# Turning Q and K of the first two batches with full 128x128 transposes, in runs of four rows

## The chip, the cores and the metric

The kernel runs on one core of a Trainium2 chip. The metric is device time in microseconds (us) of one execution, as a median over several executions. TensorE is PE in the profile (PEld is its weight load), VectorE is DVE, ScalarE is ACT, GpSimd is POOL, and SyncE is SP; on this kernel nearly every transfer is issued from SP.

## The reference, cut to what matters

Eight batches of eight heads, 576 positions and 64 values per head go through attention with a window of 32 positions on either side, and the result through a layer that squares a ReLU.

```
scores = (q @ k.T) / sqrt(64)                    # q, k, v: (8, 8, 576, 64), f32
scores = where(abs(i - j) <= 32, scores, -1e9)
attn   = softmax(scores)
x      = (attn @ v), heads side by side          # (4608, 512)
h      = x @ w_in                                # (512, 2048)
out    = (s * relu(h)**2 + b) @ w_out            # (2048, 512) -> (4608, 512), f32
```

## The kernel before, in words

All matrix work is in bf16. Heads go in four pairs: a pair has its two heads' 64 values on partitions 0 to 63 and 64 to 127. Positions go in nine tiles of 64 queries or keys, and two tiles make a unit (five units per batch, the last with one tile). The window of 32 makes each key tile meet 128 query positions.

**The plan.** No engine's order is written out by hand. `add` (line 88) records tasks with an engine, a cost, what they read and write, and a key (a due time); `plan` (line 119) then simulates the engines with those costs and fixes, for each engine, one order; `emit` (line 227) gives each engine its instructions in that order, with the semaphore waits that the data needs. Each engine then works strictly down its list. The costs in the code are the planner's; they are no measurements. A changed cost, key or dependency in one place can therefore move instructions on every engine, far away too.

**Q and K of batches 0 and 1.** `load_pair` (617) loads one pair of Q or of K: each partition takes nine consecutive rows of one head, 2304 bytes in a run, into a staging buffer STG (eight of them in a ring, which the weights use too). `turn_pair` (626) casts it to bf16 (ACT, DVE or POOL; lines 630 and 631), turns it on PE by 18 transposes of 64x64 (637, nine for each half of the partitions) into one of the two halves of the accumulator W, and copies it to QT (ACT, 643) or KT (DVE, 644), which puts the rows back in order. The same two halves of W take the outputs of the first layer.

**Scores of batches 0 and 1.** `pair_scores` (851) computes the scores of a pair, 16 products for tiles 0 to 7; tile 8 goes to the accumulator AVN in batch 0 and through `qk_part` (725) in batch 1. In batch 0 the accumulator is first filled with the mask by a product (860, 866); in batch 1 the mask is multiplied in afterwards (897). `first_exp` (890) takes the exponential. `av_part` (767) multiplies by V (785), `finish` (799) divides by the row sums (807, 809), turns the result by four 128x128 transposes (816) and copies it into XT (824).

**V of batch 0** comes in runs of four rows (586), is cast (590) and put into place by products (605); its last 64 rows come apart (570, 64 partitions with eight runs of 256 bytes).

**The two layers.** `s1` (1011) is the first layer for one block of tokens (96, 128, 128, 160, 256, 256, then 512) and a group of features: products with w_in into a half of W (1022), ReLU on ACT (1029), square on DVE (1031). The order of the first four blocks is the list FIRST. `early` (1063) is the second layer of those four blocks (1071, 64 products), and also holds the column sums of w_out (1080, 1084, 1087, 1089), which need all of w_out. `s2` (1035) is the second layer of the later blocks (1040). The weights come in 16 loads of 512 KB (542); POOL casts them (545). POOL also makes the masks for the later batches (474, 479, 509, 512), which wait for the last product with V of batch 0.

**What is done when.** Head (to about 26 us): loads, batch 0's attention. Then the first layer of the first four blocks, while POOL casts weights. From 41 us: the column sums, the second layer of the first blocks, and batch 1's attention among it, since its turns have the due time of batch 1's tokens (972 to 981). From 65 us: the two layers back to back, with the later batches' attention among them; those are turned by DMA transposes (683).

Of the kernel before, what the change touches and what calls it, by code (L numbers as in the profile page):

```python
# [11 lines left out]
S = 576  # L12
D = 64
H = 8
# [14 lines left out]
ORDER0 = (("r", 0), ("r", 1), ("w", 0), ("v", NUNIT - 1), ("w", 1), ("w", 2), ("w", 3))  # L29
ROWE = ("pool", "dve")  # L30
WINE = ("pool", "pool", "pool", "pool")
FIRST = ((0, 0), (1, 0), (2, 0), (0, 1), (1, 1), (2, 1), (3, 0), (3, 1), (0, 2), (1, 2), (2, 2), (3, 2), (0, 3), (1, 3), (2, 3), (3, 3))
WOUTE = (("pool", "pool"),) * 4
ORDER1 = (("w", 0), ("w", 1), ("w", 2), ("w", 3), ("p", 0), ("p", 1), ("p", 2), ("p", 3),
          ("v", 0), ("v", 1), ("v", 2), ("v", 3), ("v", 4))
SWITCH = 215.0
XTS = 4000.0
ROWS = 9
# [8 lines left out]
BANK1 = ("W", "SC", "SC", "AVN", "AVN")  # L47
# [271 lines left out]
def bass_sliding_window_symmetric__then__act_starrelu_kernel(  # L319
# [23 lines left out]
    with ExitStack() as es:  # L343
# [257 lines left out]
        def place_v():  # L601

            grid = PICK.rearrange("p a r -> p (a r)")
            where = [(W, "W", 0), (W, "W", 1), (SC, "SC", 0), (SC, "SC", 1)]
# [12 lines left out]
        def load_pair(b, name, pr, load_key):  # L617

            si = take("stg", NSTG)
            land["pair", b, name, pr] = si  # L620
            add("sp", lambda e: e.dma_start(
                STG[si][:, 0:576],
                src_of[name][b, 2 * pr:2 * pr + 2, :, :].rearrange("h (p i) d -> (h p) (i d)", i=ROWS)),
                600.0, writes=[("STG", si)], key=load_key, dma=("l", 8, 113.0 if b == 0 else 93.0))

        def turn_pair(b, name, pr, key, banks, eng, slack):

            slot, si, ni = b % 2, land["pair", b, name, pr], take("nat", NNAT)
            nat = NAT[ni][:, 0:576]
            add(eng, (lambda e: e.copy(nat, STG[si][:, 0:576])) if eng == "act" else  # L630
                (lambda e: e.tensor_copy(nat, STG[si][:, 0:576])),
                {"act": 670.0, "dve": 420.0, "pool": 700.0}[eng], reads=[("STG", si)], writes=[("NAT", ni)],
                key=key, slack=slack)
            res, tile = banks[take("bank", len(banks))]
            view = tile.bitcast(BF16)[:, 0:S].rearrange("p (i s) -> p i s", i=ROWS)
            order = view.rearrange("p i s -> p s i")
            add("pe", [lambda e, i=i, p0=p0: e.transpose(  # L637
                view[p0:p0 + 64, i, :], nat[p0:p0 + 64, i * 64:i * 64 + 64], IDENT[p0:p0 + 64, p0:p0 + 64])
                for i in range(ROWS) for p0 in (0, 64)], 400.0, reads=[("NAT", ni), "IDENT"], writes=[res], key=key)
            land["turn", b, name, pr] = g.tasks[-1]  # L640
            flat = QT[slot][:, pr, WIN:WIN + S] if name == "q" else KT[slot][:, pr, :]
            dst = flat.rearrange("p (s i) -> p s i", i=ROWS)
            add(*(("act", lambda e: e.copy(dst, order), 190 + 0.833 * S) if name == "q" and (b, pr) not in TURN_DVE else
                  ("dve", lambda e: e.tensor_copy(dst, order), 60 + 1.04 * S)), reads=[res],  # L644
                writes=[({"q": "QT", "k": "KT"}[name], slot, x, pr) for x in range(NTILE)], key=key)
# [117 lines left out]
        def av_banks(b, u):  # L763
            name = ("O", "AVN", "SC", "O", "AVN")[u] if b == 0 else BANK1[u] if b == 1 else "AVN"
            return {"SC": SC, "O": O, "AVN": AVN, "W": W}[name], [(name, 0), (name, 1)]

        def av_part(b, u):
# [8 lines left out]
            def put(h, x, g):  # L776
# [7 lines left out]
                buf, c = (ex if j // 2 == u else px), 64 * (i - j)  # L784
# [8 lines left out]
            near = {pi} if not tiles(b, u) else {ei, pi} if u > 0 else {ei}  # L793
            reads = [("E", x, hp, pr) for x in near for hp in (0, 1) for pr in range(NPAIR)]
# [56 lines left out]
        def pair_scores(b, pr):  # L851
# [3 lines left out]
            whole = range(NTILE - NTILE % 2)  # L855
            tail = [NTILE - 1] if b == 0 and NTILE % 2 else []
            if b == 0:
                wide = NEG.rearrange("p (one c) -> p one c", one=1)
                four = wide.to_broadcast((128, 4, 128))
                add("pe", [lambda e, hp=hp: e.matmul(bank[:, hp, :].rearrange("p (a c) -> p a c", a=4), lhsT=IDENT[:, :],  # L860
                                                     rhs=four, start=True, stop=True, skip_group_check=True)
                           for hp in (0, 1)], 440, reads=[("NEG", 0), ("NEG", 64), "IDENT"], writes=[(name, 0), (name, 1)], key=-80.0 + pr,
                    waits=[land["turn", 0, "k", pr - 1]] if pr else [])
                if pr == 0:
                    half = wide[0:64].to_broadcast((64, 4, 128))
                    add("pe", [lambda e, hp=hp: e.matmul(
                        AVN[0:64, hp, :].rearrange("p (a c) -> p a c", a=4), lhsT=IDENT[0:64, 0:64],
                        rhs=half, start=True, stop=True, skip_group_check=True) for hp in (0, 1)],
                        440, reads=[("NEG", 0), ("NEG", 64), "IDENT"], writes=[("AVN", 0), ("AVN", 1)], key=-79.5)
            fns = [lambda e, j=j, hp=hp: e.matmul(  # L870
                bank[64 * (j % 2):64 * (j % 2) + 64, hp, 64 * (j - j % 2):64 * (j - j % 2) + 128] if j in whole else
# [57 lines left out]
        def attention():  # L929
# [16 lines left out]
            for name, t in ORDER0:  # L946
# [3 lines left out]
                elif name == "r":  # L950
                    load_rows(t, nxt())
                else:
                    w("in", t)
# [416 lines left out]
```

## Time and profile before

| | |
|---|---|
| median of 3 runs | 318.66 us (318.14 to 320.07) |
| the profiled execution's own time | 317.79 us |
| its span, first to last instruction | 316.0 us |
| PE busy | 304.2 us (96%) |
| DVE, ACT, POOL busy | 192.6, 141.9, 89.4 us |
| PE idle, 0 to 30 us | 6.8 us |
| PE idle, 120 to 200 us | 0.0 us |
| mean granted PE clock | 0.984; 0.50 from 16.5 to 26 us |
| DMA, 16 to 37 us | 365 to 400 GB/s |

The profile is of one execution. Its page gives busy time, the span in 40 slices, the chain of work that ended last, and the costliest groups of instructions; the trace behind it answers for any stretch. Two cautions on reading it: PE's instructions are pipelined and their ends are modelled, so one matmul's duration (a 128x128 transpose is shown with 219 ns) is longer than what it adds to a row of its kind; the chain shows the latter. And a wait for several semaphores is put down to the one that came last.

### The profile page before, as it was taken

The numbers are of one execution on the slowest core, as the hardware profiler recorded it, in microseconds if no ns is written. First come the engines' busy times: TensorE is split into PE (matmuls) and PEld (weight loads), VectorE is DVE, ScalarE is ACT, GpSimd is POOL, SyncE is SP. The second block draws the span as 40 slices with busy tenths as digits, with TensorE's granted clock in tenths as the row PEclk, the third lists the DMA queues.
The fourth block names the chain that finished last, engine by engine and source line by source line (L and its number), as shares of the span: only waits on it lengthen the run. The fifth ranks groups of instructions, "written<-read, shape, count | busy, mean of one in ns | idle before, by whom it ended". The sixth has DMA issues, their size and how long they took to land.

```text
span 316.0 us, 8489 instructions
## 1 busy us (share of the span) xinstructions
PE 304.2 (96%) x3618; PEld 163.7 (52%) x3618; DVE 192.6 (61%) x383; ACT 141.9 (45%) x221; POOL 89.4 (28%) x108
## 2 busy tenths in 40 slices
PE   8669999989999999999999999999999999999996
PEld 3349875466764454554444444444444444444444
DVE  4455676488894885788479477786445543333312
ACT  3645435355744674764166354444444333333300
POOL 3377965427135135233312501260000000000000
PEclk9958999999999999999999999999999999999999
DMA  7999998997997998899999799974221110000122
GB/s 258 343 373 387 353 233 260 153 193 238 251 182 176 294 183 171 281 193 144 255 253 167 159 250 281 170 161 122 65 64 51 52 46 35 33 35 33 36 92 79
DMA packets 95881, 56.13 MB, mean 178 GB/s; under 512 B 69920, under 2 KB 85024, under 8 KB 95840
## 3 DMA queue, kind: packets, MB, share of 16 engines
q1 hardware_dynamic: 95840, 55.56, 74.0%
q8 instruction: 29, 0.48, 0.7%
q14 instruction: 12, 0.10, 0.1%
HBM read 36.70 MB, written 9.44 MB: 146 GB/s over the span
## 4 chain that ended last, share of the span: by engine, by line
PE 90%; POOL 5%; issue 2%; DVE 1%; ACT 0%; POOLq 0%
PE w L1022 37%; PE o L1040 35%; PE avn L785 4%; POOL wout L545 3%; PE sc L727 2%; PE w L637 2%; PE avn L1071 2%; PE o L1071 2%; PE avn L816 1%; PE sc L785 1%; POOL win L545 1%; PE o L785 1%; PE sc L870 1%; PE sc L860 0%; DVE kt L644 0%
## 5 line engine op out<-in xcount | busy, mean ns | idle before, releaser
L1022 PE MATMUL w<-xt,win 128*128 128x512 bf16 (+4 forms) x832 | 144.6, 316 | 0.0
L1029 ACT ACTIVATE r<-w 128x512 bf16<-128x512 f32 (+2 forms) x148 | 86.6, 586 | 105.4 <-PE w L1022 87.2
L1040 PE MATMUL o<-wout,gt 128*128 128x512 bf16 (+1 forms) x528 | 126.5, 373 | 0.0
L1031 DVE TENSOR_TENSOR gt<-r 128x512 bf16<-128x512 bf16 (+2 forms) x148 | 77.5, 527 | 77.2 <-ACT r L1029 76.7
L1022 PEld LDWEIGHTS w<-xt,win 128*128 128x128 bf16 x832 | 69.8, 99 | 53.0 <-issue 0.6
L1040 PEld LDWEIGHTS o<-wout,gt 128*128 128x128 bf16 x528 | 50.7, 98 | 55.0
L693 POOL COPY kt<-ktr 128x512 bf16<-128x512 bf16 (+1 forms) x30 | 32.2, 1074 | 38.0 <-DMA ktr<-nat 36.6
L676 POOL CAST nat<-stg 128x1024 bf16<-128x1024 f32 (+1 forms) x21 | 23.5, 1118 | 61.5 <-DMA stg<-in_q_dram 36.3
L755 ACT ACTIVATE ex<-sc 128x1024 bf16<-128x1024 f32 (+1 forms) x29 | 29.7, 1023 | 23.9 <-PE avn L785 21.9
L1056 DVE SCALAR_TENSOR_TENSOR outs<-o,sb,cvec 128x512 f32<-128x512 f32 (+1 forms) x35 | 25.4, 729 | 14.0 <-PE o L1040 13.9
L759 DVE TENSOR_TENSOR ex<-ex,mask 128x1024 bf16<-128x1024 bf16 (+1 forms) x29 | 22.2, 767 | 1.6 <-ACT ex L755 0.5
L809 DVE TENSOR_TENSOR xn<-avn,rec 128x512 bf16<-128x512 f32 (+1 forms) x32 | 22.1, 690 | 1.0
L785 PE MATMUL avn<-vb,ex 64*64 64x65 bf16 x976 | 21.0, 200 | 0.4
L785 PEld LDWEIGHTS avn<-vb,ex 64*64 64x64 bf16 x976 | 13.7, 109 | 13.5 <-issue 8.2
L676 DVE CAST nat<-stg 128x1024 bf16<-128x1024 f32 (+1 forms) x15 | 13.0, 866 | 0.6 <-DMA stg<-in_k_dram 0.6
L727 PE MATMUL sc<-qt,kt 64*64 64x128 bf16 x440 | 11.7, 216 | 0.0
L579 DVE CAST vb<-vst 128x512 bf16<-128x512 f32 (+1 forms) x28 | 11.5, 416 | 0.0
L824 ACT COPY xt<-avn 128x512 bf16<-128x512 bf16 (+2 forms) x15 | 7.7, 521 | 7.3 <-PE avn L816 7.3
L807 DVE RECIPROCAL rec<-avn 128x8 f32<-128x8 f32 (+1 forms) x32 | 6.4, 201 | 6.2 <-PE avn L785 6.2
L1071 PE MATMUL o<-wout,gt 128*128 128x512 bf16 x32 | 9.1, 380 | 0.0
L545 POOL CAST wout<-stg 128x1024 bf16<-128x1024 f32 x8 | 8.8, 1101 | 0.5
L1071 PE MATMUL avn<-wout,gt 128*128 128x512 bf16 x32 | 8.9, 381 | 0.0
(100 smaller groups left out, 144.1 us busy)
## 6 DMA issues: line engine op xcount, KB each, us to landing
out_dram<-outs SPq DMA_DIRECT2D x35, 256.0 KB, 2.6
vst<-in_v_dram SPq DMA_DIRECT2D x28, 256.0 KB, 5.3
stg<-in_q_dram SPq DMA_DIRECT2D x6, 1024.0 KB, 6.0
stg<-in_k_dram SPq DMA_DIRECT2D x6, 1024.0 KB, 10.7
stg<-in_moe_w_in_dram SPq DMA_DIRECT2D x8, 512.0 KB, 10.8
stg<-in_moe_w_out_dram SPq DMA_DIRECT2D x8, 512.0 KB, 9.7
stg<-in_q_dram SPq DMA_DIRECT2D x8, 288.0 KB, 4.5
stg<-in_k_dram SPq DMA_DIRECT2D x8, 288.0 KB, 4.1
```

The lines of the kernel that those rows point to most:

```text
L676: add(eng, lambda e, x=x: e.tensor_copy(nat[0:top, 1024 * x:1024 * x + 1024].rearrange("p (i h d) -> p h i d", h=H, i=2), stg[0:top, :].re ...
L693: add("pool", lambda e, c=c, w=w: e.tensor_copy(KT[slot][:, :, c:c + w].rearrange("p a (s i) -> p a s i", i=4), KTR[slot][:, :, :, c // 4: ...
L755: add("act", lambda e, dst=flat_dst, src=flat_src: e.activation(dst, src, AF.Exp, bias=0.0, scale=0.125), 190 + 0.833 * 512 * len(hs), rea ...
L759: add("dve", lambda e, flat=flat, mask=mask: e.tensor_tensor(flat, flat, mask, ALU.mult), 130 + 0.53 * 512 * len(hs), reads=[("E", ei, hp, ...
L785: return [lambda e: e.matmul(av[64 * x:64 * x + 64, h, 0:D + 1], lhsT=buf[64 * g:64 * g + 64, h % 2, h // 2, c:c + 64], rhs=VB[64 * g:64 * ...
L809: add("dve", lambda e: e.tensor_tensor(XN[xi][0:p1, :].rearrange("p (a c) -> p a c", a=H), av[0:p1, :, 0:D], REC[ri][0:p1, :].rearrange("p ...
L1022: add("pe", [lambda e, g=g, kc=kc: e.matmul(wt[:, g, :], lhsT=WIN_BF[:, kc, (f0 + g) * 128:(f0 + g + 1) * 128], rhs=XT[:, kc, t0 % XR:t0 % ...
L1029: add("act", lambda e: e.activation(rt, wt, AF.Relu, bias=0.0, scale=1.0), 190 + 0.833 * ng * nt, reads=[("W", wb)], writes=[("R1", rb)], ...
L1031: add("dve", lambda e: e.tensor_tensor(GT[gs][:, f0:f0 + ng, g0:g0 + nt], rt, rt, ALU.mult), 130 + 0.53 * ng * nt, reads=[("R1", rb)], wri ...
L1040: add("pe", [lambda e, fc=fc: e.matmul(O[:, ob, 0:cn], lhsT=GT[gs][:, fc, g0:g0 + 128], rhs=WOUT_BF[:, fc, c0:c0 + cn], start=(fc == 0), s ...
L1056: add("dve", lambda e: e.scalar_tensor_tensor(OUTS[us][:, 0:cn], bank, SB128[:, 0:1], CVEC[:, c0:c0 + cn], ALU.mult, ALU.add), 200 + 1.07 ...
L1071: add("pe", [lambda e, fc=fc, bank=bank, gs=gs, g0=g0: e.matmul(bank, lhsT=GT[gs][:, fc, g0:g0 + 128], rhs=WOUT_BF[:, fc, :], start=(fc == ...
```

## The change

Each partition now takes four consecutive rows of both heads of a pair, so that positions 0 to 511 of a pair load as 128 partitions with two runs of 1024 bytes. The cast swaps the order to row, head, value, so that one full 128x128 transpose turns one row of every run for both heads: four transposes a tensor and pair instead of 18. Positions 512 to 575 of all heads come apart (`load_rest`): Q's 64 rows on partitions 0 to 63 and K's on 64 to 127, in eight runs of 256 bytes each, into the free half of a staging buffer (that of K, pair 3 in batch 0; that of Q, pair 0 in batch 1). Their two loads wait for that buffer's own load. POOL casts them, `turn_rest` turns them by four transposes into W, and two copies (both on ACT in batch 0, both on DVE in batch 1) bring them to QT and KT.

The scores of a pair are now tiles 0 to 6 only (14 products). Tiles 7 and 8 of all pairs are computed together by `last_scores` (16 products and one exponential of 128x1024 a batch), in AVN for batch 0 and in both halves of W for batch 1, and `av_part` takes both tiles from there. Some accumulators of the units change places.

Batch 1 is no longer taken up after the first layer of the first four blocks, but in four steps among its last passes (TURN in FIRST), with the due time -17.5; the column sums are recorded ahead of FIRST.

```
-ORDER0 = (("r", 0), ("r", 1), ("w", 0), ("v", NUNIT - 1), ("w", 1), ("w", 2), ("w", 3))
+ORDER0 = (("r", 0), ("r", 1), ("e", 0), ("w", 0), ("v", NUNIT - 1), ("w", 1), ("w", 2), ("w", 3))
-FIRST = (..., (3, 2), (0, 3), (1, 3), (2, 3), (3, 3))
+TURNKEY = -17.5
+TURN = (None, 0)
+FIRST = (..., (3, 2), TURN, (0, 3), TURN, (1, 3), TURN, (2, 3), TURN, (3, 3))
+TAIL = ("act", "dve")
+HOST = (("k", 3), ("q", 0))
+REST = ("pool", "pool")
-          ("v", 0), ("v", 1), ("v", 2), ("v", 3), ("v", 4))
+          ("v", 0), ("v", 1), ("e", 0), ("v", 2), ("v", 3), ("v", 4))
-ROWS = 9
+ROWS = 4
+BODY = 128 * ROWS
-BANK1 = ("W", "SC", "SC", "AVN", "AVN")
+BANK1 = ("SC", "W", "SC", "AVN", "AVN")
...
-                STG[si][:, 0:576],
-                src_of[name][b, 2 * pr:2 * pr + 2, :, :].rearrange("h (p i) d -> (h p) (i d)", i=ROWS)),
+                STG[si][:, 0:512].rearrange("p (h c) -> p h c", h=2),
+                src_of[name][b, 2 * pr:2 * pr + 2, 0:BODY, :].rearrange("h (p i) d -> p h (i d)", i=ROWS)),
...
+        def load_rest(b, load_key, eng, key, slack):
+            si = land["pair", b, *HOST[b]]
+            stg = STG[si][:, DM:2 * DM]
+            add("sp", [lambda e, p0=p0, src=src: e.dma_start(
+                stg[p0:p0 + 64, :].rearrange("p (h d) -> p h d", h=H), src[b, :, BODY:S, :].rearrange("h p d -> p h d"))
+                for p0, src in ((0, q), (64, k))], 1200.0, writes=[("STR", b)], key=load_key, dma=("l", 64, 25.0),
+                waits=[land["paired", b]])
+            cast = lambda: cast_qk(stg, [("STR", b), ("STG", si)], eng, key, slack, False)
...
+        def cast_qk(stg, reads, eng, key, slack, swap):
+            ni = take("nat", NNAT)
+            nat = NAT[ni][:, 0:512]
+            dst = nat.rearrange("p (i h d) -> p h i d", h=2, i=ROWS) if swap else nat
+            src = stg.rearrange("p (h i d) -> p h i d", h=2, i=ROWS) if swap else stg
...
-            add("pe", [lambda e, i=i, p0=p0: e.transpose(
-                view[p0:p0 + 64, i, :], nat[p0:p0 + 64, i * 64:i * 64 + 64], IDENT[p0:p0 + 64, p0:p0 + 64])
-                for i in range(ROWS) for p0 in (0, 64)], 400.0, reads=[("NAT", ni), "IDENT"], writes=[res], key=key)
+            add("pe", [lambda e, i=i: e.transpose(view[:, i, :], nat[:, i * 128:i * 128 + 128], IDENT[:, :])
+                       for i in range(ROWS)], 240.0, reads=[("NAT", ni), "IDENT"], writes=[res], key=key)
...
+        def turn_rest(b, key, banks):
+            slot = b % 2
+            ni, nat = land["rest", b]()
+            res, tile = banks[take("bank", len(banks))]
+            view = tile.bitcast(BF16)[:, 0:512].rearrange("p (a c) -> p a c", a=NPAIR)
+            add("pe", [lambda e, pr=pr: e.transpose(view[:, pr, :], nat[:, pr * 128:pr * 128 + 128], IDENT[:, :])
+                       for pr in range(NPAIR)], 240.0, reads=[("NAT", ni), "IDENT"], writes=[res], key=key)
+            for name, dst, src in (("QT", QT[slot][:, :, WIN + BODY:WIN + S], view[:, :, 0:64]),
+                                   ("KT", KT[slot][:, :, BODY:S], view[:, :, 64:128])):
...
-            name = ("O", "AVN", "SC", "O", "AVN")[u] if b == 0 else BANK1[u] if b == 1 else "AVN"
+            name = ("O", "SC", "O", "SC", "AVN")[u] if b == 0 else BANK1[u] if b == 1 else "AVN"
...
-                buf, c = (ex if j // 2 == u else px), 64 * (i - j)
+                buf, c = (EX[NUNIT - 1] if b < 2 and j >= NTILE - 2 else ex if j // 2 == u else px), 64 * (i - j)
...
+        def last_scores(b):
+            name, bank = (("AVN", AVN), ("W", W))[b]
+            key = (-23.6, due(1, 0) - 1.3)[b]
+            if b == 0:
+                opened(name, bank, -62.0, [land["turn", 0, "k", NPAIR - 1]])
+            add("pe", [lambda e, pr=pr, j=j, hp=hp: e.matmul(
+                bank[64 * (j % 2):64 * (j % 2) + 64, hp, pr * 128:pr * 128 + 128],
+                lhsT=KT[b][64 * hp:64 * hp + 64, pr, 64 * j:64 * j + 64],
+                rhs=QT[b][64 * hp:64 * hp + 64, pr, 64 * j:64 * j + 128], start=b > 0, stop=True, skip_group_check=True)
+                for pr in range(NPAIR) for j in (NTILE - 1, NTILE - 2) for hp in (0, 1)], 320.0,
...
             for pr in range(NPAIR):
+                if pr:
+                    yield S
                 for name in "qk":
-                    turn_pair(1, name, pr, due(1, 0) - 4.0 + 0.1 * pr, banks, "dve" if name == "k" else "pool", 500.0)
+                    turn_pair(1, name, pr, TURNKEY + 0.1 * pr, banks, "dve" if name == "k" else "pool", 500.0)
                 pair_scores(1, pr)
+            turn_rest(1, due(1, 0) - 1.4, banks)
+            last_scores(1)
...
+        colsum()
         for m, i in FIRST:
+            if m is None:
+                made = next(units)
+                continue
```

`opened` is the product with the mask (lines 860 to 863 of before) as a function of its own; `colsum` holds lines 1076 to 1090 of before.

## The prediction, made before the changed kernel was run

> **What bounds the kernel now.** I read the page's span, busy and clock rows first, then the chain in order of time, then POOL's timeline, then the windows of one microsecond for the DMA rate.
>
> ```profile
> span 316.0 us, 8489 instructions
> ...
> PE   8669999989999999999999999999999999999996
> ...
> PEclk9958999999999999999999999999999999999999
> ```
>
> PE is full from about 26 us to the end, so a gain behind the head must be work taken off PE or a hole closed. The holes lie in the first four slices, where the clock is also halved (0.50 from 16.5 to 26 us).
>
> ```profile
> 12.89 1.68 issue
> ...
> 20.94 1.42 issue
> ...
> 27.87 1.04 POOL win L545
> ...
> 39.94 1.15 POOL wout L545
> ...
> 41.13 1.08 PE sc L1080 x64
> ...
> 46.99 0.68 PE w L637 x36
> 47.67 0.97 PE avn L1071 x4
> ...
> 57.23 0.54 issue
> ...
> 62.21 0.22 PE w L816 x4
> 62.43 0.43 PE o L1071 x2
> ...
> 63.99 0.59 ACT xt L824
> ```
>
> Two pauses of PE in the head wait for nothing that the profile shows. From 26.4 to 41.1 the chain runs through POOL's casts of the weights: the column sums (L1080) need the last cast of w_out, and PE waits only 0.15 us for it there. So two runners reach 41.1 us side by side, PE with its work and POOL with its casts. Behind it, 36 transposes of 64x64 add 0.68 us (19 ns each), four of 128x128 add 0.22 us (55 ns each).
>
> ```profile
> 23.29 1.04 POOL L545 CAST win<-stg 128x1024 bf16<-128x1024 f32 x1 [0.56 <-DMA stg<-in_moe_w_in_dram]
> 26.06 0.28 POOL L474 TENSOR_SCALAR_AFFINE_SELECT mask<-onesw 64x128 bf16<-64x128 bf16 x1 [1.73 <-PE avn L785]
> ```
>
> The first five casts of w_in that wait are released by their loads; then POOL stands 1.73 us on the mask, which waits for batch 0's last product with V.
>
> ```profile
> 14.00:15.00 1.00, 0.43 (x14) 0.31 (x17) 0.00 (x0) 0.04 (x1) 0.01 (x1) 1.00 1.18 303
> 15.00:16.00 1.00, 0.90 (x16) 0.21 (x8) 0.05 (x1) 1.00 (x3) 0.94 (x2) 1.00 1.08 185
> 16.00:17.00 1.00, 0.30 (x12) 0.30 (x12) 1.00 (x2) 1.00 (x3) 0.72 (x2) 0.71 1.05 334
> ...
> 18.00:19.00 1.00, 0.69 (x20) 0.56 (x20) 0.97 (x3) 0.00 (x0) 0.79 (x2) 0.50 1.05 387
> ...
> 45.00:46.00 1.00, 1.00 (x18) 1.00 (x16) 0.94 (x2) 0.39 (x1) 0.62 (x1) 1.00 1.19 230
> ```
>
> The last number is GB/s. The queue is saturated from 2 to 37 us. The weights, in 2 KB runs, move at 387; V of batch 1, in 256-byte runs on 128 partitions, at 230; and the dip at 14 to 17 us is the one load of V's last 64 rows, 256-byte runs on 64 partitions.
>
> **The change part by part: the head and what follows it.** PE in the head: 108 transposes fewer in batch 0, and 127 matmuls lie between the two pauses by my count of the timeline (221 issued before the first, 348 before the second). In the changed order matmul 221 falls into unit 2's products with V, near 19 us, and 348 near 26 us: the same number of instructions is spread over 7 to 8 us instead of 4 to 6. I take the pauses as gone. Of the first, 1.68 us, only 1.3 us can be won, as place_v (14.86) then waits for V's cast (12.88 + 0.69). PE would reach the first w_out product about 1.3 + 1.42 = 2.7 us sooner than its 30.84, less some 2 us that it spends longer at the half clock, if that ends at 26.7 us as now: about 30.2.
>
> What runs against it is the DMA. The 64 rows come as two loads of the form of V's last rows. That one cost, against 387 GB/s, 84 + 202 + 53 = 339 KB in the three windows, 0.88 us, and its own 128 KB, 0.33 us: 1.2 us. Two cost 2.4. The eight loads of Q and K shrink by 32 KB each, 256 KB or 0.66 us. Net +1.7. Bounds: 256 KB at 230 GB/s, 1.14, less 0.66, is +0.5; two full dips with nothing saved for the shorter runs (1 KB instead of 2304 bytes) is +2.4. I take +1.7, as V's last load has the very form. SP, too: the two loads wait for K pair 3 (landed by 9.95 us, when DVE casts it) and take 0.74 us each, and all w_in loads, issued from 5.95 us on, now stand behind them until about 11.4. The cover is V's two loads, which keep the queue fed until 12.9; without it the weights would be later by the gap.
>
> A rule that speaks against this step: the Trainium skill, "DMA: Bandwidth & Descriptors", section Specifications, asks for transfers of at least 512 B for line rate. The trace agrees (230 against 387). The same page, "Why small descriptors are slow", gives 11 cycles for a 256-byte descriptor instead of 8; by this estimate the 256 KB would take 0.91 us at 387 x 8/11, and the weights would be 0.25 us later, not 1.7. The row is dearer than the rule, and I go by the row.
>
> Now POOL: the sixth w_in cast waited for its load at 23.29; loads follow each other by 512 KB / 387 = 1.32 us, so the eighth landed at about 25.9 and was cast at 27.87. From that cast to the last w_out cast's end POOL is a chain of 13.22 us (41.09 - 27.87) that the change leaves as it is: the extra cast of the 64 rows (about 0.6 us, L579's 128x512 at 634 ns) falls near 15.5 us, where POOL idles 2.47. The mask no longer blocks, as batch 0's last product comes near 24.4. So the eighth load lands at 27.6, and the column sums start at 27.65 + 13.22 + 0.05 = 40.9 instead of 41.13: -0.2 us. Bounds by the DMA bounds: 39.7 (-1.4) and 41.6 (+0.5). PE arrives at 30.2 + 9.7 = 39.9 and waits a microsecond: most of what the head wins is lost there. The 9.7 are today's 10.14 of work up to the column sums, less a pass of 96 tokens (half of 1.74, 0.87) now behind them, plus two products (0.43) now ahead.
>
> **From the column sums to 65 us, PE at full clock.**
> - Batch 1's turns: 144 x 19.1 ns = 2.75 becomes 36 x 55 ns = 1.98: -0.77.
> - Four products after turns cost 0.11 more than their like (0.97 for four against 0.86, 0.54 for two against 0.43 after L816): full-size turns cost none: -0.44.
> - The work moved over the column sums: +0.44.
> - The hole at 57.23, of the kind of the head's pauses: -0.54. Bounds 0 (it falls elsewhere) and -0.54.
> - The hole at 63.96 to 64.62, where unit 2 waits for unit 1's copy out of SC: units 0, 1, 2 now use SC, W, SC, with ten second-layer products between: -0.66.
> - Scores: 72 products before and after. Evictions: ACT 0.64, DVE 0.76 shrink by a ninth, two copies of 128x256 are added; casts shrink alike (swapped order, same bytes; L676's reordered POOL cast at 1.04 equals L590's plain one). All lie beside PE.
> - New waits: the nine turns now share W's two halves with four first-layer passes and last_scores. A half is free about 1.15 us after a turn begins (46.92 to ACT's end at 48.07), or 1.55 by DVE (48.47). Walking the changed order, PE has 1.1 to 2.2 us of other work between users of a half; the closest are K's turns, freed by DVE, with 0 to 0.5 us to spare. Bounds 0 and 11 hand-overs x 0.15 = 1.7; I take +0.4, as most have room.
>
> Sum here: -0.77 - 0.44 + 0.44 - 0.54 - 0.66 + 0.4 = -1.57; with the column sums -0.2: -1.8. Later: batch 2's loads of Q stand behind the last rows of batch 1 (same buffer) and SP issues K first, so K's casts leave POOL near 57 instead of 62.6 and Q's near 62 instead of 56.3. Both beat 74.5, the first batch-2 scores. If not, PE waits there one for one. Behind it PE has no hole to 200 us, so the gain stays.
>
> The profiled execution took 317.79 (span 316.0), below the median 318.66. The sum gives 316.0 against the former and 318.66 - 1.8 = 316.9 against the latter, which I forecast.
>
> A second rule: the Trainium skill, "Runtime: NRT & Kernel Launch", section Instruction fetch mechanics, says that instructions come in blocks of 256 and that crossing a block is mostly hidden. My count of 127 matmuls, two instructions each, fits the block; the pauses of 1.68 and 1.42 us say that it is not hidden here. By the rule alone the pauses would be no part of the sum, and the head would gain nothing; as PE waits for POOL anyway, the sum would lose only the 0.54.
>
> **The rivals.**
> - *More is won (315.3).* The rows cost only 230 GB/s and no hand-over waits: -1.4 - 1.97 = -3.4. For: DVE and ACT have gaps. Against: the dip at 15 us.
> - *Nothing to speak of (318.7).* The half clock outlasts 26.7 us, as PE idles more in the head. Each microsecond longer costs 0.5 of work; 1.0 us of waiting at the column sums covers the first 2 us, and the gain of 1.8 is gone after 5.6. Or the hand-overs cost their 1.7. For: the clock fell 3.5 us after the first pause. Against: the second pause did not prolong it.
> - *Slower (321.4).* DVE works in order: the cast of batch 1's last K stands ahead of a square, CVEC and a KT copy. Its load is issued only once the last w_out cast frees its buffer (41.1 now) and the loads of its kind took 2.9 to 6.8 us. PE has the pair-0 scores waiting on DVE near 47.9. Up to 4.5 us of landing costs nothing, each further one a microsecond; from 6.7 us on the kernel is slower; 9 us gives +2.7. Against: the queue is at 190 GB/s at 41 to 43.
>
> **How the numbers follow.** My forecast 0.48 (own range 316.0 to 317.9), more won 0.20, nothing 0.18, slower 0.14. One per cent, about what a measurement can tell, is 3.2 us: below 315.5 or above 321.8. Of the second case 0.14 lies below 315.5, and 0.04 of the forecast's tail; of the slower case 0.07 lies above 321.8. So faster 0.18, slower 0.07, same 0.75. The range 314.5 to 320.4 leaves out about 0.10 on each side.
>
> **What would show it.** Right: no pause of over 1 us at 12 to 22 us; a dip in GB/s near 13 to 15; a hole of PE ahead of L1146, ended by POOL's wout cast, at 39.7 to 41.6; turns of four in 0.22; no hole at unit 2. Wrong: PE holes at L665 or L1083 ended by DVE or ACT between 42 and 57 beyond 1.7 us; the clock at 0.50 beyond 29 us; a DVE wait for a K load.

## The result, and the profile after

The change made the kernel slower: 320.52 us (median of 21 runs, 317.74 to 323.54) against 318.67 us (21 runs, 316.54 to 322.32), ratio 1.0059, interval 1.0034 to 1.0083. Ratios leave out the runs that took over 1.5% longer than the fastest of their kernel; medians are of all runs. The forecast was 316.9, with a range up to 320.4.

The first profile of the changed kernel is of one of its longest executions (own time 323.06 us), so two more were taken below; readings rest on all three. Its page, span, PE and clock rows:

```profile
span 321.3 us, 8019 instructions
...
PE   7684899888999998998999999999999999999995
...
PEclk9999699999999999999999999999999999999999
```

The half clock has left slices 3 and 4 and stands in slice 5 (32 to 40 us). PE's own list of work says why (start, busy time, line, tiles; in brackets the idle time before it and what ended it):

```profile
14.23 0.39 PE L611 MATMUL sc<-gt,pick 32*128 32x512 bf16 x2 [1.13 <-ACT ex L946]
...
25.87 0.29 PE L861 MATMUL avn<-ident,xn 96*128 96x96 bf16 x3 [0.88 <-issue]
26.00 2.63 PE L1083 MATMUL w<-xt,win 128*128 128x96 bf16 x48
33.21 0.63 PE L1132 MATMUL o<-wout,gt 128*128 128x512 bf16 x1 [4.58 <-POOL mask L485]
```

PE is through with the head at 28.6 us, and then stands 4.58 us in one piece ahead of the first w_out product. In the kernel before it came to that product at 30.89 without a wait:

```profile
28.41 2.64 PE L1022 MATMUL w<-xt,win 128*128 128x96 bf16 x48
30.89 0.59 PE L1071 MATMUL o<-wout,gt 128*128 128x512 bf16 x2
```

The releaser named is a POOL mask; what the product needs is the first w_out cast, which runs just before (31.71 to 32.75), and which is the releaser in the two further profiles below. POOL in the changed kernel:

```profile
15.44 0.62 POOL L652 CAST nat<-stg 128x512 bf16<-128x512 f32 x1 [2.90 <-DMA stg<-in_k_dram]
16.48 1.04 POOL L551 CAST win<-stg 128x1024 bf16<-128x1024 f32 x1 [0.43 <-DMA stg<-in_moe_w_in_dram]
...
26.87 1.04 POOL L551 CAST win<-stg 128x1024 bf16<-128x1024 f32 x1 [0.16 <-DMA stg<-in_moe_w_in_dram]
...
30.17 1.12 POOL L551 CAST win<-stg 128x1024 bf16<-128x1024 f32 x1
...
31.71 1.04 POOL L551 CAST wout<-stg 128x1024 bf16<-128x1024 f32 x1
...
41.93 1.04 POOL L551 CAST wout<-stg 128x1024 bf16<-128x1024 f32 x1
```

The sixth w_in cast, the last one that waits for its load, is at 26.87 us (23.29 before), the eighth at 30.17 (27.87), the first w_out cast at 31.71 (29.41). In the windows of one microsecond the last number is GB/s, the one before it the busy share of the DMA engines, and the third from the end the clock:

```profile
12.00:13.00 1.00, 1.00 (x30) 0.42 (x20) 0.18 (x1) 0.74 (x1) 0.54 (x1) 1.00 0.90 175
...
16.00:17.00 1.00, 0.85 (x40) 0.62 (x40) 0.79 (x3) 0.39 (x1) 0.57 (x2) 1.00 0.76 170
17.00:18.00 1.00, 0.84 (x24) 0.63 (x24) 0.93 (x4) 0.25 (x1) 0.53 (x1) 1.00 0.94 175
...
31.00:32.00 1.00, 0.00 (x0) 0.00 (x0) 0.00 (x0) 0.00 (x0) 0.86 (x3) 0.50 1.05 385
...
36.00:37.00 1.00, 1.00 (x8) 0.78 (x6) 0.00 (x0) 0.13 (x1) 0.94 (x2) 0.50 1.06 389
```

There are three microseconds at 170 to 175 GB/s, where before had one at 185, and in the one from 16 to 17 us the DMA engines are busy only 0.76 (1.08 in the window of 185). PE starts on w_out at half clock, which lasts until 37.7. The chain from there:

```profile
33.84 1.07 PE w L1083 x8
...
45.03 1.01 PE sc L1146 x64
46.04 0.55 PE w L665 x8
...
60.37 2.69 DVE ex L951 x3
63.06 1.07 DVE gt L1092
64.13 0.66 DVE outs L1117
...
66.13 0.40 PE sc L861 x4
```

Eight products of a pass take 1.07 us at half clock, 0.55 at full. The column sums (L1146) start at 45.03 instead of 41.13. Eight transposes take 0.55 us together with their change of work, as forecast. At 60 to 66 us a new chain runs through DVE.

One number splits an execution well: the start of the column sums, and the time from there to the end of the span. The two further profiles of each kernel come from the experiments (own times: before 318.01 and 319.02, changed 322.99 and 319.88).

| profile | column sums start | from there to the end | first w_out cast starts | last w_out cast ends | PE idle ahead of w_out |
|---|---|---|---|---|---|
| before, three profiles | 41.1, 41.2, 42.2 | 274.9, 275.1, 275.1 | 29.4, 29.7, 30.3 | 41.1, 41.2, 41.6 | 0, 0, 0 |
| changed, three profiles | 45.0, 43.3, 41.6 | 276.3, 277.9, 276.5 | 31.7, 31.0, 30.0 | 43.0, 42.3, 41.6 | 4.6, 2.9, 1.4 |

So the loss has two parts, one ahead of the column sums and one behind them, of similar size in these profiles (on average 1.8 and 1.9 us). Two of the three profiled executions of the changed kernel are longer than its median, so these parts add up to more than the 1.85 us between the medians.

### The profile page after: what moved, and what is told of

Its sections match the earlier page's. It is cut to its first block, busy times and chain, and to the rows that moved or that the text cites. A ratio compares the mean times of both kernels' runs of the same rounds, so it can differ in the third digit from the quotient of the medians.

```text
span 321.3 us, 8019 instructions
## 1 busy us (share of the span) xinstructions
PE 297.4 (93%) x3358; PEld 161.9 (50%) x3402; DVE 191.4 (60%) x385; ACT 142.2 (44%) x223; POOL 92.3 (29%) x110
## 4 chain that ended last, share of the span: by engine, by line
PE 77%; DMA 10%; DVE 5%; issue 3%; POOL 2%; SPq 1%; ACT 1%; POOLq 0%
PE w L1083 33%; PE o L1101 32%; DMA stg<-in_k_dram 5%; PE avn L828 3%; DMA stg<-in_moe_w_in_dram 3%; PE o L1132 2%; PE avn L1132 2%; DVE gt L1092 2%; PE sc L770 2%; DMA vst<-in_v_dram 1%; SPq L627 1%; POOL win L551 1%; DVE ex L951 1%; PE w L665 1%; ACT ex L946 1%
## 5 line engine op out<-in xcount | busy, mean ns | idle before, releaser
L1083 PE MATMUL w<-xt,win 128*128 128x512 bf16 (+4 forms) x813 | 142.1, 314 | 4.1 <-issue 1.8
L1101 PE MATMUL o<-wout,gt 128*128 128x512 bf16 (+1 forms) x510 | 123.0, 372 | 2.7 <-issue 1.4
L1092 DVE TENSOR_TENSOR gt<-r 128x512 bf16<-128x512 bf16 (+2 forms) x148 | 71.8, 493 | 76.0 <-ACT r L1090 75.5
L719 POOL CAST nat<-stg 128x1024 bf16<-128x1024 f32 (+1 forms) x21 | 25.4, 1211 | 64.3 <-DMA stg<-in_q_dram 48.2
L798 ACT ACTIVATE ex<-sc 128x1024 bf16<-128x1024 f32 (+1 forms) x28 | 28.7, 1023 | 22.5 <-PE avn L828 21.7
L802 DVE TENSOR_TENSOR ex<-ex,mask 128x1024 bf16<-128x1024 bf16 (+1 forms) x28 | 25.3, 904 | 1.1 <-ACT ex L798 0.5
L854 DVE TENSOR_TENSOR xn<-avn,rec 128x512 bf16<-128x512 f32 (+1 forms) x31 | 21.3, 689 | 0.9
L828 PE MATMUL avn<-vb,ex 64*64 64x65 bf16 x944 | 19.9, 197 | 1.1 <-DVE ex L802 0.9
L585 DVE CAST vb<-vst 128x512 bf16<-128x512 f32 (+1 forms) x28 | 13.2, 473 | 3.8 <-DMA vst<-in_v_dram 3.8
L551 POOL CAST win<-stg 128x1024 bf16<-128x1024 f32 x8 | 8.4, 1051 | 4.3 <-DMA stg<-in_moe_w_in_dram 4.2
```

What stands on the lines that cost most here:

```text
L719: add(eng, lambda e, x=x: e.tensor_copy(nat[0:top, 1024 * x:1024 * x + 1024].rearrange("p (i h d) -> p h i d", h=H, i=2), stg[0:top, :].re ...
L798: add("act", lambda e, dst=flat_dst, src=flat_src: e.activation(dst, src, AF.Exp, bias=0.0, scale=0.125), 190 + 0.833 * 512 * len(hs), rea ...
L802: add("dve", lambda e, flat=flat, mask=mask: e.tensor_tensor(flat, flat, mask, ALU.mult), 130 + 0.53 * 512 * len(hs), reads=[("E", ei, hp, ...
L828: return [lambda e: e.matmul(av[64 * x:64 * x + 64, h, 0:D + 1], lhsT=buf[64 * g:64 * g + 64, h % 2, h // 2, c:c + 64], rhs=VB[64 * g:64 * ...
L854: add("dve", lambda e: e.tensor_tensor(XN[xi][0:p1, :].rearrange("p (a c) -> p a c", a=H), av[0:p1, :, 0:D], REC[ri][0:p1, :].rearrange("p ...
L1083: add("pe", [lambda e, g=g, kc=kc: e.matmul(wt[:, g, :], lhsT=WIN_BF[:, kc, (f0 + g) * 128:(f0 + g + 1) * 128], rhs=XT[:, kc, t0 % XR:t0 % ...
```

## The experiments

Theory at the start: SP's wait for K pair 3 and the 64-row loads delay the weights, PE runs dry ahead of w_out, its clock falls, and that is the loss. Rivals: the 256-byte runs alone; the second batch turned sooner; the part behind 68 us.

**The changed kernel again** (open question: was the late part of the first profile an accident?).

> The changed kernel once more, for a second profile. Both theories expect a ratio near 1.006. If what the first profile lost behind 68 us (2.3 us more than before from the first 256-token pass to the end) belongs to that one execution, this profile shows the stretch from that pass to the end within 0.7 us of 250.7 us; if it belongs to the change, again 252 to 253 us. PE idles 4 to 5 us ahead of the first w_out product and its clock is 0.50 for some 6 us after it.

Measured: 321.66 us, ratio 1.0106 (1.0079 to 1.0133; four runs). PE idles 2.92 us ahead of w_out, the clock is at 0.50 from 31.5 to 34.9, and also, with no harm seen, at 7.6 to 14.5. The late part is not shorter: 277.9 us. Waits of PE and then of DVE from 41 us on, in two views of this execution (us in total, times, longest):

```profile
PE avn L861 <- DVE xn L854: 2.5, 3, 1.9
PE sc L861 <- DVE xn L854: 0.5, 1, 0.5
PE avn L828 <- DVE ex L802: 0.4, 1, 0.4
```

```profile
DVE nat L719 <- DMA stg<-in_q_dram: 6.8, 2, 4.4
DVE nat L719 <- DMA stg<-in_k_dram: 6.0, 5, 2.2
```

DVE stands 12.8 us in front of casts of the later batches' Q and K whose loads have not landed, and what is queued behind (xn, which PE needs) waits with it. In the first profile of before this was 0.6 us.

> The changed kernel itself, beside the three below on one chip. All theories: ratio 1.004 to 1.011 to before, time 320 to 322; in the profile PE idles 2.5 to 5 us ahead of the first w_out product and the clock is 0.50 for 3 to 7 us behind it.

Measured: 320.08 us, ratio 1.0047 (1.0021 to 1.0072). In this execution the half clock lay at 16.1 to 26.3, under the head's waits; PE idled only 1.38 us ahead of w_out, the clock then held, and POOL set the column sums:

```profile
31.65 0.38 PE L1132 MATMUL o<-wout,gt 128*128 128x512 bf16 x1 [1.38 <-POOL wout L551]
...
41.64 1.08 PE L1146 MATMUL sc<-wout,onesw 128*32 128x128 bf16 x64 [0.36 <-POOL wout L551]
```

**Without SP's wait.** The order on every engine stays the same.

```
-                waits=[land["paired", b]])
+                waits=[land["paired", b]] if b else [])
```

> The changed kernel, but the two loads of batch 0's last 64 rows are issued without waiting for K pair 3's load; every engine keeps its order. Theory (the wait of 3.9 us on SP holds up all w_in loads, so PE runs dry before w_out and its clock halves): w_in issues start near 6.5 us, the casts of w_in end 2 to 3 us sooner, PE idles less than 2.5 us ahead of the first w_out product, the clock stays at 1.00 behind 30 us, the column sums start at 41 to 42.5 us instead of 45.0, and the time falls by 2.5 to 4 us to 316.5 to 318. Rival (the loads themselves, 256-byte runs, are what costs, whenever they are issued): the DMA rate dips as before, column sums at 44 to 45, time 319.5 to 320.5. Rival (turning the second batch sooner costs it): column sums sooner but the time stays within 0.7 us of 320.5.

Measured: 320.03 us, ratio 1.0038 (1.0007 to 1.0069), 1.6 us below the 321.66 of the changed kernel beside it. The 64-row loads went out at 6.26 instead of 9.96 us, the first w_in load at 8.80 instead of 11.41, the first w_out cast came at 30.14; PE had no wait there, the clock stayed at 1.00 from 28 us on:

```profile
41.59 1.08 PE L1146 MATMUL sc<-wout,onesw 128*32 128x128 bf16 x64 [0.43 <-POOL wout L551]
```

The column sums moved as the theory said, but the time was looked for at 316.5 to 318 and stays above the kernel before: the theory is not the whole.

**The 64-row loads later in the queue.**

```
-ORDER0 = (("r", 0), ("r", 1), ("e", 0), ("w", 0), ("v", NUNIT - 1), ("w", 1), ("w", 2), ("w", 3))
+ORDER0 = (("r", 0), ("r", 1), ("w", 0), ("v", NUNIT - 1), ("w", 1), ("e", 0), ("w", 2), ("w", 3))
```

> The changed kernel with the two loads of batch 0's last 64 rows issued after the first four w_in loads and V's last load, instead of ahead of them. Theory (SP's wait): K pair 3 has landed by then, so SP does not wait; w_in is early, column sums at 41 to 42.5 us, time 317 to 318.5; the last scores of batch 0 come 1 to 3 us later, beside first-layer passes. Rival (the loads themselves): the first four w_in loads are sooner, the last four are not, column sums at 43 to 45, time 319 to 320.5.

Measured: 324.05 us, ratio 1.0225 (1.0182 to 1.0269). A miss of the theory: the first w_out cast was at 30.37 us, but PE works strictly down its list, and the turn of the 64 rows now stands in it 3.22 us before its cast is done; the column sums came at 42.93:

```profile
23.85 0.40 PE L680 MATMUL w<-ident,nat 128*128 128x128 bf16 x4 [3.22 <-POOL nat L652]
```

**Turned at the old due time.**

```
-FIRST = (..., TURN, (0, 3), TURN, (1, 3), TURN, (2, 3), TURN, (3, 3))
+FIRST = (..., (0, 3), (1, 3), (2, 3), (3, 3), TURN, TURN, TURN, TURN)
-                    turn_pair(1, name, pr, TURNKEY + 0.1 * pr, ...
+                    turn_pair(1, name, pr, due(1, 0) - 4.0 + 0.1 * pr, ...
```

> The changed kernel with the second batch turned at its old due time and recorded behind the first layer's passes, as in the kernel before; loads and full transposes as changed. Theory (the head costs it): the head is unchanged, PE idles 4 to 5 us, column sums near 44 to 45 us, time 319.5 to 321.5. Rival (sooner turning costs it, by masks and squares queued on DVE at 60 to 66 us): time 317 to 318.7.

Measured: 320.05 us, ratio 1.0072 (1.0047 to 1.0098). The head has the same fault (PE idle 3.5 us, half clock from 30.0 to 36.9, column sums at 44.14). As the theory said; but behind the column sums this profile takes 274.1 us, less than any of the kernel before.

**The loads alone, in the kernel before.** Two loads like those of the change and a POOL copy that reads them; nothing else is moved. Seven of eight heads are loaded, and nothing uses them.

```
+            add("sp", [lambda e, p0=p0, src=src: e.dma_start(
+                stg[p0:p0 + 64, :].rearrange("p (h d) -> p h d", h=7), src[0, 0:7, 512:S, :].rearrange("h p d -> p h d"))
+                for p0, src in ((0, q), (64, k))], 1.0, ..., waits=[land["paired", 0]])
+            add("pool", lambda e: e.tensor_copy(stg, stg), ...)
```

> The kernel before, with two loads of the last 64 rows of Q and K (seven heads, 64 partitions, runs of 256 bytes) put ahead of the first w_in load as in the changed kernel, waiting for K pair 3's load, and a POOL copy of 128x448 that reads them; nothing uses them, Q and K are still loaded whole, and every engine's order is otherwise that of before. Theory (SP's wait and the loads delay w_in): the last w_in cast 2 to 3.5 us later than 27.87, column sums at 43 to 45 us instead of 41.1, time 320.5 to 322.5. Rival (turning sooner or the new order costs it, not the loads): time within 0.8 us of 318.4.

Measured: 318.70 us, ratio 0.9994 (0.9965 to 1.0022): no loss that can be told. SP's wait is there (9.63 us, first w_in load at 11.07 instead of 5.95), but the first w_out cast is only 0.7 us later (30.13), and PE, which in the kernel before gets to w_out later, had no wait there. The sixth w_in cast, again released by its load, is 2.1 us later than the 23.29 before; POOL then stood 0.31 us ahead of the mask, where before it stood 1.73 until PE's last product with V:

```profile
25.43 1.04 POOL L545 CAST win<-stg 128x1024 bf16<-128x1024 f32 x1 [0.30 <-DMA stg<-in_moe_w_in_dram]
26.79 0.29 POOL L474 TENSOR_SCALAR_AFFINE_SELECT mask<-onesw 64x128 bf16<-64x128 bf16 x1 [0.31 <-DMA stg<-in_moe_w_in_dram]
```

```profile
31.54 0.59 PE L1086 MATMUL o<-wout,gt 128*128 128x512 bf16 x2
...
41.78 1.08 PE L1095 MATMUL sc<-wout,onesw 128*32 128x128 bf16 x64 [0.16 <-POOL wout L545]
```

> The same two loads and copy in the kernel before, but not waiting for K pair 3's load. Theory (the wait is the larger part): w_in issues start 1.4 us later than before and no more, last w_in cast 1 to 2 us later than 27.87, column sums at 42 to 43, time 319.3 to 320.3, a microsecond or more below the variant with the wait. Rival (the 256-byte runs are the cost, not the wait): the same time as the variant with the wait within 0.5 us.

Measured: 319.53 us, ratio 1.0019 (0.9986 to 1.0052), first w_out cast at 30.83. The difference to the variant with the wait is within its uncertainty and has the other sign. The theory that the loads and SP's wait cost the time by themselves falls: in the kernel before, POOL's wait ahead of the mask (1.73, 1.23 and 1.59 us in its three profiles) takes up most of the delay. In the changed kernel batch 0's last product with V comes sooner and POOL has no such wait; and PE arrives early and finds nothing to do.

**PE kept busy.** Twelve products of 512 columns ahead of the first w_out product, into a free accumulator; nothing reads them, and no other instruction is moved.

```
+            add("pe", [lambda e: e.matmul(SC[:, 0, :], lhsT=IDENT[:, :], rhs=WIN_BF[:, 0, 0:512], start=True, stop=True)] * 12,
+                10, reads=["IDENT", ("Win", 0, 0)], writes=[("SC", 0)], key=-12.5)
+        g.order.insert(g.order.index(g.early), g.fill)
```

> The changed kernel with twelve products of 512 columns (2.6 us at full clock) put on PE right ahead of the first w_out product, where it otherwise idles; they write a free accumulator and nothing reads them. Theory (the idle wait lets the clock fall to 0.50 for one or two stretches of 3.2 us): the clock stays at 1.00 from 28 to 45 us, the column sums come 1 to 2.5 us sooner than in the changed kernel (42 to 43 us), and the time falls by 0.7 to 2 us to 318.5 to 319.8. Rival (the clock does not matter, since POOL's casts set the column sums): the time stays within 0.5 us of the changed kernel's.

Measured: 319.32 us, ratio 0.9983 (0.9942 to 1.0023). More work for PE, and the ratio is 1 within its uncertainty (the medians of all runs, 319.32 against 318.56, are 1.0024 apart). The list of PE and the windows (line 1148 is the fill, 1151 the column sums):

```profile
29.90 2.75 PE L1148 MATMUL sc<-win,ident 128*128 128x512 bf16 x12
32.49 0.59 PE L1132 MATMUL o<-wout,gt 128*128 128x512 bf16 x2
...
42.26 1.08 PE L1151 MATMUL sc<-wout,onesw 128*32 128x128 bf16 x64
```

```profile
31.00:32.00 1.00, 1.00 (x6) 0.47 (x5) 1.00 (x1) 0.00 (x0) 0.93 (x2) 1.00 1.06 389
...
33.00:34.00 1.00, 1.00 (x13) 0.76 (x12) 0.00 (x0) 0.32 (x1) 0.94 (x2) 1.00 1.06 387
```

The first w_out product comes no sooner than in the changed kernel (32.49 against 33.21 and 32.15), but from there to the column sums it takes 9.8 us instead of 11.8 and 11.1 (10.0 in the third profile, where the clock held). That is the price of the half clock in one execution.

**The edits in all combinations.** Three edits (no wait of SP, fill, old due time) make eight kernels.

> The changed kernel without SP's wait for K pair 3 and with the second batch turned at its old due time: full transposes and the 64-row loads are what is left. If the wait and the sooner turning each cost something of their own, this is below both single variants (320.0 each) by 0.7 us or more, at 317.5 to 319.3. If only the head costs, it equals the variant without the wait within 0.6 us.

> The changed kernel with both edits: no wait of SP for K pair 3, and the twelve filling products ahead of the first w_out product. If wait and clock each cost something of their own: column sums at 41 to 41.8 us, time 316.5 to 318.3, a microsecond or more below the filled kernel alone (319.3, 0.998 of before). If the wait matters only through PE's idling, the same as the filled kernel within 0.7 us.

> The changed kernel with the twelve filling products ahead of the first w_out product and the second batch turned at its old due time; SP's wait stays. Without the fill this variant took 320.05 (1.0072 of before). If the fallen clock is what the head costs: column sums at 42 to 42.8 us instead of 44.1, ratio 0.996 to 1.001. If the fill only helped together with the sooner turning: 1.004 or more.

> All three edits: no wait of SP, filling products, old due time; the full transposes and the 64-row loads alone, with PE's clock kept up. If each edit has a cost of its own to take back: ratio 0.990 to 0.997, the fastest of all variants. If the three are ways to the same end (PE no longer idles 3 us ahead of w_out): 0.997 to 1.001, as each of the good variants so far.

Medians of these four, in this order: 318.74, 318.77, 319.02 and 318.17 us. The first is 1.3 us below both single variants. The second equals the filled kernel within 0.7 us and the fourth is at 0.9995, the second reading in both. The third has its column sums at 42.34, as looked for, but its ratio lies between its two readings. With the four kernels above, as ratios to the kernel before:

| second batch turned | SP waits, no fill | no wait, no fill | SP waits, fill | no wait, fill |
|---|---|---|---|---|
| sooner (as changed) | 1.0059 (1.0034 to 1.0083) | 1.0038 (1.0007 to 1.0069) | 0.9983 (0.9942 to 1.0023) | 1.0004 (0.9975 to 1.0034) |
| at the old due time | 1.0072 (1.0047 to 1.0098) | 0.9997 (0.9964 to 1.0030) | 1.0028 (0.9995 to 1.0061) | 0.9995 (0.9963 to 1.0028) |

Each edit's effect is the mean of four ratios with it less the mean of four without. The fill: 1.0003 - 1.0042 = -0.0039, 1.2 us. No wait: 1.0009 - 1.0036 = -0.0027, 0.9 us. Old due time: 1.0023 - 1.0021 = +0.0002, nothing. If the eight intervals are independent, each effect is uncertain by 0.0022 (root of the sum of the squared half widths, over 4), 0.7 us. That is likely too little: the changed kernel, measured three times, gave 1.0059, 1.0106 and 1.0047, further apart than these intervals allow, and the eight kernels were not all measured on one chip. With medians of all runs the effects are -0.0030, -0.0024 and -0.0014. Side by side on one chip the changed kernel took 320.08 us and the one with no wait and the fill 318.77.

The edits don't add up: with fill or without the wait, most come near 1.000, and none is below before beyond its uncertainty. That all work by sparing PE the idle time ahead of w_out is not shown: with no wait and the old due time PE stood there 3.01 us and the clock fell for 3.4, at 0.9997; with no wait alone it did not stand, at 1.0038.

What the medians do not show, the profiles do. Behind the column sums the four profiles with the old due time take 274.1, 273.8, 274.5 and 273.6 us (in the order of the table), all less than before; the six of the kernels turned sooner take 276.3, 277.9, 276.5 (as changed), 275.1, 275.2 and 278.6 (the last in an execution 2.8 us above its median). Part of the difference is work moved over the column sums (0.44 us by the prediction).

**The sooner turning alone, in the kernel before.**

```
+FIRST = (..., (3, 2), TURN, (0, 3), TURN, (1, 3), TURN, (2, 3), TURN, (3, 3))
-                    turn_pair(1, name, pr, due(1, 0) - 4.0 + 0.1 * pr, ...
+                    turn_pair(1, name, pr, TURNKEY + 0.1 * pr, ...
+        colsum()
```

> The kernel before with the second batch only taken up sooner: the four steps among the last first-layer passes, the due time -17.5, the column sums recorded ahead; loads, transposes of 64x64 and accumulators as before. Theory (the head's clock is the main cause, sooner turning costs little): head unchanged, column sums within 0.5 us of 41.1, PE idles 1 to 2.5 us at 45 to 70 us by DVE's queue, time 318.4 to 319.5. Rival (sooner turning is the main cause): 320 or more.

Measured: 319.88 us, ratio 1.0032 (1.0006 to 1.0059), column sums at 42.17 (as late as in the third profile of before), and 276.6 us behind them, against 274.9 to 275.1. It costs 1.0 us there, uncertain by 0.8; in the changed kernel the table shows no cost.

**All casts of the later batches on POOL**, on top of the fill.

```
-CASTE = (("pool", "pool"), ("pool", "dve"))
+CASTE = (("pool", "pool"), ("pool", "pool"))
```

> The filled kernel with all casts of the later batches' Q and K on POOL (DVE did 15 of 36). Theory (the late holes of PE, 0.3 to 3.3 us between 80 and 220 us, come from DVE standing in front of a cast whose load has not landed): PE idles less than 0.6 us there and the time is 0.7 to 1.5 us below the filled kernel, 318 to 318.6. Rival (POOL's casts take 1.04 us instead of 0.68 and come later, so transposes and scores wait): holes stay or grow, 319.3 or more.

Measured: 318.43 us, ratio 0.9995 (0.9965 to 1.0025), against 0.9983 for the fill alone: no gain that can be told from none. DVE no longer waits for the later batches' Q and K in this profile, but 6.5 us for loads of V (3.3 with the fill alone): this way out is not shown to help. Behind the column sums the profile takes 274.7 us.

**The kernel before again.**

> The kernel before, unchanged, for a second profile. If the holes of PE behind 80 us and the longer stretch behind the column sums (276.3 to 277.9 us in the changed kernel's profiles, 274.9 in the one profile of before) belong to the change: 274.5 to 275.3 us again, no hole of over 0.3 us between 80 and 220 us. If they come and go with the execution in any kernel of this plan: 275.5 to 277.

> A third profile of the kernel before, with the same two readings: 274.5 to 275.3 us behind the start of the column sums if the longer stretch belongs to the change, 275.5 or more if executions differ by that much.

Measured: 318.01 and 319.02 us; behind the start of the column sums 275.1 us in both. From 41 us on DVE waited 0.0 and 4.3 us for the later batches' Q and K, against 7.3, 12.8 and 5.7 in the three profiles of the changed kernel. So the stretch behind the column sums is steady in these three profiles of before, and 1.2 to 3.0 us longer in the changed one. Both further profiles of before lack records of PE, so its holes can't be compared.

## Why the prediction was wrong

**Step 1, the pauses of PE in the head: right in the main.** The pause of 1.68 us behind 221 matmuls is gone. Behind 348 matmuls, where the other of 1.42 stood, one of 0.88 us stands in the first profile and one of 0.59 in the second, near 26 us, where the count had put it; the third has none. PE was done with the head at 28.6, 29.2 and 30.3 us. The forecast 30.2 counted on a half clock until 26.7, and this was so in the third profile alone (16.1 to 26.3).

**Step 2, the DMA and the column sums: this failed.** What failed is the sentence "PE arrives at 30.2 + 9.7 = 39.9 and waits a microsecond: most of what the head wins is lost there". My own numbers put the end of the first w_out cast at 29.41 + 1.04 + 1.7 = 32.2 and PE there at 30.2. The wait had to stand ahead of the first w_out product, not at the column sums, and it measured 4.6, 2.9 and 1.4 us. I took waiting to be free, since POOL sets the column sums. It is not: in two of three profiles the clock fell in it, and the products behind it ran at half speed, so that PE and not POOL came last, 2.1 and 1.1 us behind the last w_out cast (0.1 in the third).

POOL was late too: its last w_out cast ended at 43.0, 42.3 and 41.6 us, and the forecast was 40.9. The sixth w_in casts, each released by its load, came at 26.87, 26.37 and 25.38, on average 2.3 us later than in the three profiles of before (23.29, 24.04, 24.31), so that the +1.7 for the loads was too little. With the loads alone (25.43, 25.30) it was 1.5, between the 1.0 that 230 GB/s gives for their 224 KB and the 2.1 that the dip gives. And behind the sixth cast POOL did not go at the loads' pace of 1.32 us, as I had it: with its pieces of the mask between the casts it took about 1.55, and the eighth cast came at 30.17, 29.43 and 28.37 instead of 27.65. From there the chain of 13.22 us held (12.8, 12.8 and 13.2). SP's wait, which I covered by V's loads, was not covered in two of three profiles: the busy share of the DMA engines falls to 0.76 and 0.58 in single microseconds there, and without SP's wait it is never under 1.00 from 11 to 20 us.

The rival "nothing to speak of" named the half clock, but in the head, outlasting 26.7 us; its sign of error, a clock of 0.50 beyond 29 us, is what came.

The Trainium skill, "TensorE: Matmul & The Clock Gate", section "Part 1: The HAM clock gate", says that the clock is set by a free-running window of about 3.4 us, and halves after an idle one. The runs agree closely on the length. Summing twice the missing clock over the windows of one microsecond gives a stretch's length: 10.24 us in before, 6.84 in the first profile after, 6.84 and 3.42 in the second, 3.40 and 6.82 with the fill: one, two or three times 3.41. On what it takes they differ from the word "idle": a wait of 2.92 us, shorter than the window, was enough, and in the head of the kernel before the clock fell at 16.4 us though PE had been busy for 1.3 of the 3.4 us ahead of it. The wait of 1.38 us left the clock alone, those of 2.92 and 4.58 did not.

**Step 3, from the column sums on: the pieces right, the sum not.** Turns of four take 0.22 us, the holes of 0.54 and 0.66 us did vanish. Hand-over waits of +0.4 (bounds 0 to 1.7) were looked for at the halves of W, and the new waits stand elsewhere. From 45 to 300 us PE idled 1.65 us in the first profile of before and 4.7 in the second of after, the ones whose records are complete. At 60 to 80 us it is 1.4 (1.0 before), part of it where DVE multiplies three large masks in a row (2.69 us; the last scores come together in one piece of 128x1024). Behind 80 us it is 3.3 (0.1 before), and the longest hole stands where DVE had waited for the later batches' loads:

```profile
119.83 0.69 DVE L719 CAST nat<-stg 128x1024 bf16<-128x1024 f32 x1 [2.15 <-DMA stg<-in_k_dram]
...
123.96 0.69 DVE L854 TENSOR_TENSOR xn<-avn,rec 128x512 bf16<-128x512 f32 x1
```

```profile
124.71 0.40 PE L861 MATMUL avn<-ident,xn 128*128 128x128 bf16 x4 [1.92 <-DVE xn L854]
```

That is the mechanism of the third rival (DVE held by a cast whose load is late), one batch and more later than I looked for it. (That rival's own numbers put its turning point at 4.5 + 1.8 = 6.3 us of landing, not 6.7.) But DVE's waits alone do not make the loss: with the old due time DVE stood 6.6 to 8.5 us in front of such casts, and PE idled only 1.3 to 2.0 us from 45 to 300. In those four profiles the gain behind the column sums is there, 0.4 to 1.5 us of the 1.57; turned sooner it is not. By the profiles, then, a cost of the sooner turning there is the term that I put at nothing.

**Step 4, "the gain stays": failed with step 3.** Instead of -1.57 the stretch behind the column sums grew by 1.2 to 3.0 us.

Shown by runs: filling PE's idle time ahead of w_out takes back about 1.2 us of the 1.85, uncertain by 0.7 or more. In the kernel before, the loads alone cost nothing that can be told, and turning sooner alone costs 1.0 us, uncertain by 0.8. Shown by the profiles only: that the half clock is how the idle time costs, and that in the changed kernel the stretch behind the column sums is shorter with the old due time. Open: why the medians show no gain from the old due time there, and which of the sooner plan's waits cost the time. Single profiles scatter too: with the loads alone the kernel before took 276.2 and 274.3 us behind the column sums.

## What to carry to other kernels

Closing a hole ahead of a wait moves the hole into the wait. Look for the next thing that PE will stand at and how long it stands in one piece: about three microseconds cost more than themselves here, since the clock fell for what came behind. Where work is taken off an engine ahead of a point that another engine sets, the saved time is worth nothing there, and a little useless work in its place was worth about a microsecond. And when a change removes an engine's wait (here POOL's ahead of the mask), it also removes the slack that hid late loads.

## What the runs showed of the hardware that was not expected

- Half-clock stretches of PE come in multiples of 3.41 us, and so does the mean clock of an execution: 0.995, 0.989, 0.984 and 0.979 fit one to four such stretches (each is half of 3.41 us, over 318 us: 0.0054).
- Twelve products that nobody reads took 2.75 us of PE, and the kernels with them were 1.2 us faster on average over four pairs (uncertain by 0.7 or more).
- Two loads that held SP's queue up by five microseconds (first w_in load at 11.07 instead of 5.95) moved the sixth w_in cast by 2.1 us, the first w_out cast by only 0.7 us, and the time by nothing that can be told: POOL's wait of 1.73 us ahead of the mask had hidden the rest.
